# First feed-forward layer: Strassen products accumulated in the banks of the first and fifth product, with snapshots by ScalarE

## The chip, the core and the metric

The kernel runs on one core of a Trainium2 chip. The metric is the device time of one execution in microseconds (us); lower is better. The engines are named as the profile names them: PE is TensorE (matmuls; PEld its weight loads), DVE is VectorE, ACT is ScalarE, POOL is GpSimd, and SP is the queue that issues most DMAs. SBUF is the memory on the core from which the engines work; PSUM is the small memory into which TensorE writes its results, in eight banks of 512 fp32 values for each of 128 partitions.

## The reference

Attention within hash buckets for 4 batches x 8 heads x 768 tokens x 64, then a two-layer feed-forward network over 3072 tokens:

```python
mask = q_bucket[:, :, :, None] == k_bucket[:, :, None, :]
scores = np.where(mask, scale * np.matmul(q, k.transpose(0, 1, 3, 2)), -1000000000.0)
attn = softmax(scores)                       # over the keys
x = (attn @ v).transpose(0, 2, 1, 3)         # to (3072, 512)
h = x @ w_in                                 # w_in is (512, 2048)
g = h * (1.0 / (1.0 + np.exp(-1.702 * h)))
out = g @ w_out                              # w_out is (2048, 512)
```

The change is in the line that computes `h`, and in how `g` is taken from it. All arithmetic is fp32.

## The kernel before

**Three stages.** Attention fills `xT`, the transposed input of the network, until 316 us. Then the first layer runs until 605 us and writes `g` and sums of it to DRAM (`g_dram`). The second layer reads them back with `fetch` into `raw_g` and a part of `s_in`, and ends at 868 us.

**The first layer.** Tokens are cut in three blocks of 1024 (`sb`), the 2048 columns of `w_in` in eight pairs of 128 (`mt`). One call of `hidden(sb, mt)` makes one tile, that is, four results of 128 x 512: `u` (c11), `c12`, `c21` and `c22`, a 2 x 2 block product. It is made in the manner of Strassen and Winograd, with seven products instead of eight. Product `i` multiplies the weight quarter `LEFT[i]` with the token quarter `RIGHT[i]`; quarters 0 to 3 are parts of `w_in_sb` or `xT`, quarters 4 to 6 sums of them (`s_in` on the weights' side, `t_x` on the tokens' side). `K2` is 2, and in the profile each fp32 matmul of the program appears as two instructions, so a product is four matmul instructions of 128 x 128 x 512.

**The results of a tile**, with p1 to p7 for the products:

```
u   = p1 + p2
v   = p1 + p6
c21 = v + p7 + p4
c22 = v + p7 + p5
c12 = v + p5 + p3
```

Before the change every product has a PSUM bank of its own, which `bank()` hands out from a pool of six (`f0`; two more, `f1`, are added from tile 21 on; tiles are counted from 0 to 23). ScalarE copies p1 to `u`, and VectorE makes the other sums, each with one operand from PSUM. Then `emit` applies the activation on ScalarE (`Gelu_apprx_sigmoid`, L732) and `keep` issues the store to DRAM (L729). After the four results, POOL makes four sums for the next layer (`sums_b`, L219 to L222), which are stored too.

**What else runs in a tile.** `mid` and `end` are lists of steps that are put into the order of the engines within a tile: the sums of tokens for the next block (`sums_b(nc.vector, *quarters_x(sb + 1))`, L219 to L222 on VectorE), the conversion of `w_out` from its 64-bit form (L180 to L198 on VectorE, with a Square on ScalarE at L190, reading `raw`, which a DMA at L162 loads), sums of `w_out` quarters in the last block (`sums_a`, L211 to L214, on VectorE and POOL), and the first loads and sums of the second layer (`fetch`, L791; `g_sums`).

**What sets the order.** TensorE, VectorE, ScalarE and POOL run their instructions in the order in which the program issues them (`manual_schedule`). The DMAs on SP are put in order by a planner, by the times at which it expects their conditions to be met. Buffers of the pool `stage` (`u`, `v`, `c12`, `c21`, `c22`) exist twice, `t2` and `t4` once.

The first tile, `hidden(0, 0)`, is issued from the end of attention (`next(ff)`), before the last normalization of `xT`.

Of the kernel before, what the change touches and what calls it, by code (L numbers as in the profile page):

```python
# [8 lines left out]
F32 = mybir.dt.float32  # L9
# [3 lines left out]
Act = mybir.ActivationFunctionType  # L13
Alu = mybir.AluOpType
# [5 lines left out]
P = 128  # L20
# [18 lines left out]
def kernel(  # L39
# [17 lines left out]
    nc = tc.nc  # L57
# [8 lines left out]
    KC, FC = DM // P, FF // P  # L66
# [149 lines left out]
    def sums_b(eng, b11, b12, b21, b22, t1, t2, t4):  # L216


        return [lambda: eng.tensor_tensor(t1, b12, b11, op=Alu.subtract),  # L219
                lambda: eng.tensor_tensor(b12, b22, b12, op=Alu.subtract),  # L220
                lambda: eng.tensor_tensor(t2, b22, t1, op=Alu.subtract),  # L221
                lambda: eng.tensor_tensor(t4, b21, t2, op=Alu.subtract)]  # L222

    K2, F2 = KC // 2, FF // 2
    XT = 512

    def quarters_in(cols):
        w = [w_in_sb[:, K2 * k : K2 * (k + 1), F2 * i + cols.start : F2 * i + cols.stop]
             for i in range(2) for k in range(2)]
        return w + [s_in[:, i, :, cols] for i in range(3)]  # L230

    def quarters_x(sb):
        x = [xT[:, K2 * k : K2 * (k + 1), (2 * sb + j) * XT : (2 * sb + j + 1) * XT] for k in range(2) for j in range(2)]
        return x + [t_x[:, i] for i in range(3)]
# [460 lines left out]
    def feed_forward(tag, late=()):  # L695
# [4 lines left out]
        n1 = N // (2 * XT)  # L700

        LEFT = dict(zip(range(1, 8), (0, 1, 6, 3, 4, 5, 2)))
        RIGHT = dict(zip(range(1, 8), (0, 2, 3, 6, 4, 5, 1)))
        OUTER = (1, 2, 6, 7, 5, 3, 4)
        with ExitStack() as fctx:
            stage_ctx = fctx.enter_context(ExitStack())
            stage = stage_ctx.enter_context(tc.tile_pool(name=f"stage{tag}", bufs=2, side="right"))
# [4 lines left out]
            def bank():  # L712
                turn[0] += 1
                return sets[turn[0] % 8 // 6 if len(sets) > 1 else 0].tile([P, XT], F32, tag="p", name="product")

            def hidden(sb, mt, mid=(), end=()):
                u, v, c12, c21, c22 = (stage.tile([P, XT], F32, tag=x, name=x) for x in ("u", "v", "c12", "c21", "c22"))
                t2, t4 = (stage.tile([P, XT], F32, tag=x, name=x, bufs=1) for x in ("t2", "t4"))
                wq, xq = quarters_in(slice(mt * P, (mt + 1) * P)), quarters_x(sb)

                def product(i):
                    ps = bank()
                    for kc in range(K2):
                        nc.tensor.matmul(ps, wq[LEFT[i]][:, kc, :], xq[RIGHT[i]][:, kc, :],  # L724
                                         start=(kc == 0), stop=(kc == K2 - 1))
                    return ps

                def keep(at, x):
                    loader[0].dma_start(out=g_dram[len(LEFT) * sb + at, :, mt, :], in_=x)  # L729

                def emit(c, at=None):
                    nc.scalar.activation(c, c, Act.Gelu_apprx_sigmoid)  # L732
                    if at is not None:
                        keep(at, c)

                nc.scalar.copy(u, product(1))
                nc.vector.tensor_tensor(v, product(6), u, op=Alu.add)
                nc.vector.tensor_tensor(c21, product(7), v, op=Alu.add)
                p = product(5)
                nc.vector.tensor_tensor(c22, p, c21, op=Alu.add)  # L740
                emit(c22, 3)
                nc.vector.tensor_tensor(c12, p, v, op=Alu.add)
                nc.vector.tensor_tensor(u, product(2), u, op=Alu.add)
                emit(u, 0)
                for x in mid:
                    x()
                nc.vector.tensor_tensor(c12, product(3), c12, op=Alu.add)
                emit(c12)
                nc.vector.tensor_tensor(c21, product(4), c21, op=Alu.add)
                emit(c21, 2)  # L750

                for f, kept in zip(sums_b(nc.gpsimd, u, c12, c21, c22, v, t2, t4), ((4, v), (1, c12), (5, t2), (6, t4))):
                    f()
                    keep(*kept)
                for x in end:
                    x()
# [129 lines left out]
            for sb in range(n1):  # L886
                for mt in range(MT):
                    n = sb * MT + mt
# [36 lines left out]
                    x = sums_b(nc.vector, *quarters_x(sb + 1)) if mt == MT - 1 and sb + 1 < n1 else []  # L925
                    t = {3 * MT - 2: g_sums(0)[:2], 3 * MT - 1: g_sums(0)[2:]}.get(n, []) if n > 3 * MT - 3 else []
                    hidden(sb, mt, x[:3] + ([lambda: fetch(1)] if n == 3 * MT - 1 else []), x[3:] + t + todo.pop(n, []))
                    yield
            stage_ctx.close()
# [58 lines left out]
    def whole(steps):  # L988
        for _ in steps:
            pass  # L990

    ff = feed_forward("", in_chunks[len(in_chunks) - LATE :])
    attention(ff)
    whole(ff)
# [5 lines left out]
    with tc.If(unsafe, preferred_fallthrough_block=False):  # L1000
        with tc.tile_pool(name="cv3", bufs=1) as cv:
            for x in in_chunks:
                whole(convert(cv, *x))
        for f in in_sums(0):
            f()
        shifted_attention()
        for f in sums_b(nc.vector, *quarters_x(0)):
            f()
        whole(feed_forward("2"))
# [27 lines left out]
```

## Time and profile before

| | |
|---|---|
| median of 3 runs | 870.38 us (870.25 to 870.49) |
| span of the profiled execution | 868.1 us; no own time is shown beside it |
| mean granted clock of TensorE | 0.996 |
| first layer | 316.4 to 605.2 us |
| one product of the first layer | 4 matmuls, start to start 1.717 us |
| copy of a product by ScalarE (L736) | 24 times, mean 583 ns |
| activation of a result (L732) | 96 times, mean 630 ns |
| add with one operand from PSUM on VectorE (L737 to L749) | 7 x 24 times, 681 to 692 ns |
| sum of two SBUF operands of 128 x 512 on POOL (L219 to L222) | means 1311 to 1388 ns in the first layer |

A row of the timeline has the start, the duration, the engine, the line of the kernel, the operation with its result and operands, and in brackets for how long the engine was idle before it and which instruction ended that. Matmuls overlap in the pipeline, so that four of them that start 0.429 us apart are shown as 1.88 us.

### The profile page before, as it was taken

Reading aid. Unit: us, or ns where it says so; the run is one execution under the profiler, and the core shown is the slowest. Engines: PE = TensorE matmul, PEld = TensorE weight load, DVE = VectorE, ACT = ScalarE, POOL = GpSimd, SP = SyncE. Lnnn points to the kernel's source line nnn. Section 1 sums busy time; section 2 is a strip of 40 time slices with the busy share of each in tenths; the row PEclk is TensorE's granted clock in tenths of the full one; section 3 lists DMA queues with packets and bytes.
Section 4 is the critical chain, followed back from the end, with each engine's and each line's share of the span. In section 5 each row is a group of like instructions: output and inputs, shape, how many; then the busy total and the mean of one; then the engine's idle time right before and its main releaser. Section 6 shows DMA issues by size and latency. Waiting matters only on the chain.

```text
span 868.1 us, 13473 instructions
## 1 busy us (share of the span) xinstructions
PE 857.6 (99%) x4845; PEld 499.7 (58%) x4845; DVE 719.2 (83%) x1020; ACT 313.4 (36%) x519; POOL 313.6 (36%) x275
## 2 busy tenths in 40 slices
PE   9999999999999999999999999999999999999996
PEld 5444444444444444444444444444888888888885
DVE  4589999999999887778777778888888977897786
ACT  5866667777666643322233322332000000000000
POOL 4243223334323566665544344659904100000000
PEclk9999999999999999999999999999999999999998
DMA  5636645446552205556455555575844685467524
GB/s 126 97 56 109 107 85 85 85 89 122 98 101 61 62 2 188 186 196 212 175 195 186 189 193 194 194 251 180 301 161 154 201 246 197 162 208 242 194 98 100
DMA packets 169162, 132.10 MB, mean 152 GB/s; under 512 B 123616, under 2 KB 138112, under 8 KB 163712
## 3 DMA queue, kind: packets, MB, share of 16 engines
q1 hardware_dynamic: 166528, 129.70, 52.3%
q10 hardware_dynamic: 2560, 1.46, 0.8%
q8 instruction: 40, 0.66, 0.3%
q14 instruction: 34, 0.28, 0.1%
HBM read 79.69 MB, written 50.33 MB: 150 GB/s over the span
## 4 chain that ended last, share of the span: by engine, by line
PE 97%; DVE 2%; DMA 0%; issue 0%; ACTq 0%; ACT 0%; DVEq 0%
PE product L724 33%; PE product L836 27%; PE ps L432 18%; PE av L465 15%; PE dn L486 1%; PE hash L408 1%; DVE xT L840 1%; PE tp L366 1%; DVE y L816 1%; DMA k<-in_k_dram 0%; PE hash L373 0%; DVE v L840 0%; DVE t2a L221 0%; DVE raw_g L220 0%; ACTq L823 0%
## 5 line engine op out<-in xcount | busy, mean ns | idle before, releaser
L433 ACT ACTIVATE e<-ps 128x768 f32<-128x768 f32 x192 | 151.2, 812 | 25.6 <-PE ps L432 23.0
L432 PE MATMUL ps<-qT,kT 64*128 64x384 f32 x768 | 155.1, 482 | 0.0
L724 PE MATMUL product<-xT,w_in_sb 128*128 128x512 f32 x288 | 135.5, 593 | 0.0
L465 PE MATMUL av<-e,v 128*32 128x385 f32 x1536 | 128.0, 487 | 0.0
L440 POOL TENSOR_TENSOR acc<-e 128x768 f32<-128x768 f32 x32 | 51.8, 1619 | 194.4 <-ACT e L433 174.9
L732 ACT ACTIVATE c<-c 128x512 f32<-128x512 f32 x72 | 45.4, 630 | 186.6 <-issue 78.5
L724 PEld LDWEIGHTS product<-xT,w_in_sb 128*128 128x128 f32 x288 | 54.7, 190 | 69.0 <-issue 64.4
L465 PEld LDWEIGHTS av<-e,v 128*32 128x32 f32 x1536 | 48.6, 109 | 76.2 <-issue 73.8
L724 PE MATMUL product<-t_x,s_in 128*128 128x512 f32 x192 | 90.2, 592 | 0.0
L432 PEld LDWEIGHTS ps<-qT,kT 64*128 64x128 f32 x768 | 68.0, 188 | 38.5 <-issue 38.4
L219 POOL TENSOR_TENSOR v<-c,u 128x512 f32<-128x512 f32 x24 | 34.2, 1423 | 122.3 <-ACT c L732 122.3
L849 ACT COPY u<-product 128x256 f32<-128x256 f32 x21 | 7.8, 372 | 172.1 <-PE product L836 138.9
L432 PE MATMUL ps<-qf,kf 64*128 64x384 bf16 x384 | 62.9, 324 | 0.1
L724 PEld LDWEIGHTS product<-t_x,s_in 128*128 128x128 f32 x192 | 36.5, 190 | 45.9 <-issue 43.3
L441 POOL TENSOR_TENSOR acc<-acc,e 128x768 f32<-128x768 f32 x32 | 55.9, 1746 | 2.5
L446 DVE SCALAR_TENSOR_TENSOR acc<-e 128x768 f32<-128x768 f32 x32 | 47.7, 1492 | 5.1 <-ACT e L433 5.1
L724 PE MATMUL product<-xT,s_in 128*128 128x512 f32 x96 | 45.1, 592 | 0.0
L724 PE MATMUL product<-t_x,w_in_sb 128*128 128x512 f32 x96 | 45.1, 592 | 0.0
L432 PEld LDWEIGHTS <-kf 64*128 64x128 bf16 x384 | 19.0, 94 | 35.1 <-DMA q<-in_q_dram 6.2
L448 DVE TENSOR_TENSOR acc<-acc,e 128x768 f32<-128x768 f32 x32 | 34.3, 1072 | 3.3
L448 DVE TENSOR_TENSOR acc<-acc,acc 128x768 f32<-128x768 f32 x32 | 31.2, 974 | 6.3 <-POOL acc L441 3.2
L836 PE MATMUL product<-raw_g,xT 128*128 128x256 f32 x152 | 35.1, 379 | 0.0
(207 smaller groups left out, 1498.5 us busy)
## 6 DMA issues: line engine op xcount, KB each, us to landing
raw_g<-g_dram SPq DMA_DIRECT2D x22, 1024.0 KB
s_in<-g_dram SPq DMA_DIRECT2D x20, 1024.0 KB
g_dram<-c SPq DMA_DIRECT2D x72, 256.0 KB
g_dram<-t SPq DMA_DIRECT2D x48, 256.0 KB
raw<-in_moe_w_in_dram SPq DMA_DIRECT2D x16, 512.0 KB
raw<-in_moe_w_out_dram SPq DMA_DIRECT2D x16, 512.0 KB
v<-in_v_dram SPq DMA_DIRECT2D x32, 192.0 KB
g_dram<-u SPq DMA_DIRECT2D x24, 256.0 KB
```

Of the source, the lines that this page charges most:

```text
L219: return [lambda: eng.tensor_tensor(t1, b12, b11, op=Alu.subtract), lambda: eng.tensor_tensor(b12, b22, b12, op=Alu.subtract), lambda: eng ...
L366: nc.tensor.matmul(tp[D * j : D * (j + 1), i * P : (i + 1) * P], x[name][:, j, c * GT + i, :], ident, start=True, stop=True)
L432: nc.tensor.matmul(ps[:, j, 0:HS], a[hs, keys], m[hs, cols], start=not last, stop=last)
L433: nc.scalar.activation(es[c][:, kt, :, 0:HS], ps[:, :, 0:HS], Act.Exp, scale=1.0 / D**0.5)
L440: nc.gpsimd.tensor_tensor(acc, es[c][:, 0, :, 0:HS], es[c][:, 1, :, 0:HS], op=Alu.add)
L441: nc.gpsimd.tensor_tensor(acc, acc, es[c][:, 2, :, 0:HS], op=Alu.add)
L446: nc.vector.scalar_tensor_tensor(acc, e[0], T * TINY, e[1], op0=Alu.add, op1=Alu.add)
L448: nc.vector.tensor_tensor(acc, acc, x, op=Alu.add)
L465: nc.tensor.matmul(av[D * j + d : D * j + d + 32, :], vt[:, t, j, d : d + 32], es[c][:, t, j, :], start=(t == 0), stop=(t == T - 1))
L724: nc.tensor.matmul(ps, wq[LEFT[i]][:, kc, :], xq[RIGHT[i]][:, kc, :], start=(kc == 0), stop=(kc == K2 - 1))
L732: nc.scalar.activation(c, c, Act.Gelu_apprx_sigmoid)
L836: nc.tensor.matmul(ps, wq[LEFT[i]][:, c, :], gq[RIGHT[i]][:, c, :], start=(c == 0), stop=(c == F4 - 1))
```

## The change

The products no longer have a bank each. Product 1 starts bank `a`; product 6, then 7, then 4 are accumulated on top of it, and ScalarE takes a snapshot between them: after p1 (`u`), after p6 (`v`) and after p7 (into `c22`). The activation of c21 reads bank `a` itself. Product 5 starts bank `b`, and product 3 is accumulated onto it. Product 2 has a bank `c`. VectorE is left with three adds out of PSUM per tile: c22, u and c12. Product 1 of a tile and its copy are issued by `head`, in the middle of the tile before, except for the very first tile. The order of products was 1, 6, 7, 5, 2, 3, 4; it becomes 6, 5, 7, 2, product 1 of the next tile, 4, 3. The activation of c21 now comes before that of c12.

```diff
+            def product(ps, sb, mt, i, start=True):
+                wq, xq = quarters_in(slice(mt * P, (mt + 1) * P)), quarters_x(sb)
+                for kc in range(K2):
+                    nc.tensor.matmul(ps, wq[LEFT[i]][:, kc, :], xq[RIGHT[i]][:, kc, :],
+                                     start=(start and kc == 0), stop=(kc == K2 - 1), skip_group_check=not start)
+
+            def head(n):
+                ps, u = bank(), stage.tile([P, XT], F32, tag="u", name="u")
+                product(ps, *divmod(n, FC // 2), 1)
+                nc.scalar.copy(u, ps)
+                return ps, u
+
+            heads = {}
+
             def hidden(sb, mt, mid=(), end=()):
...
+                n = sb * (FC // 2) + mt
+                a, u = heads.pop(n) if n in heads else head(n)
...
-                def emit(c, at=None):
-                    nc.scalar.activation(c, c, Act.Gelu_apprx_sigmoid)
+                def emit(c, at=None, of=None):
+                    nc.scalar.activation(c, c if of is None else of, Act.Gelu_apprx_sigmoid)
                     if at is not None:
                         keep(at, c)
 
-                nc.scalar.copy(u, product(1))
-                nc.vector.tensor_tensor(v, product(6), u, op=Alu.add)
-                nc.vector.tensor_tensor(c21, product(7), v, op=Alu.add)
-                p = product(5)
-                nc.vector.tensor_tensor(c22, p, c21, op=Alu.add)
+                product(a, sb, mt, 6, False)
+                nc.scalar.copy(v, a)
+                b = bank()
+                product(b, sb, mt, 5)
+                product(a, sb, mt, 7, False)
+                nc.scalar.copy(c22, a)
+                nc.vector.tensor_tensor(c22, b, c22, op=Alu.add)
                 emit(c22, 3)
-                nc.vector.tensor_tensor(c12, p, v, op=Alu.add)
-                nc.vector.tensor_tensor(u, product(2), u, op=Alu.add)
+                c = bank()
+                product(c, sb, mt, 2)
+                nc.vector.tensor_tensor(u, c, u, op=Alu.add)
                 emit(u, 0)
+                if n + 1 < n1 * (FC // 2):
+                    heads[n + 1] = head(n + 1)
                 for x in mid:
                     x()
-                nc.vector.tensor_tensor(c12, product(3), c12, op=Alu.add)
+                product(a, sb, mt, 4, False)
+                emit(c21, 2, a)
+                product(b, sb, mt, 3, False)
+                nc.vector.tensor_tensor(c12, b, v, op=Alu.add)
                 emit(c12)
-                nc.vector.tensor_tensor(c21, product(4), c21, op=Alu.add)
-                emit(c21, 2)
```

More of the change, by code (lines that the diff above doesn't have):

```diff
@@ L716, in hidden @@
+            heads = {}
             def hidden(sb, mt, mid=(), end=()):
-                u, v, c12, c21, c22 = (stage.tile([P, XT], F32, tag=x, name=x) for x in ("u", "v", "c12", "c21", "c22"))
+                n = sb * (FC // 2) + mt
+                a, u = heads.pop(n) if n in heads else head(n)
+                v, c12, c21, c22 = (stage.tile([P, XT], F32, tag=x, name=x) for x in ("v", "c12", "c21", "c22"))
                 t2, t4 = (stage.tile([P, XT], F32, tag=x, name=x, bufs=1) for x in ("t2", "t4"))
-                wq, xq = quarters_in(slice(mt * P, (mt + 1) * P)), quarters_x(sb)
@@ L721, in product @@
[L721 to L726, printed above, removed]
                 def keep(at, x):
                     loader[0].dma_start(out=g_dram[len(LEFT) * sb + at, :, mt, :], in_=x)
-                def emit(c, at=None):
-                    nc.scalar.activation(c, c, Act.Gelu_apprx_sigmoid)
+                def emit(c, at=None, of=None):
+                    nc.scalar.activation(c, c if of is None else of, Act.Gelu_apprx_sigmoid)
```

## The prediction

> **What bounds the kernel now.** I read the page first, parts 1 and 4, and then the busy time of the three stages: attention, first layer (316.4 to 605.2 us), second layer.
>
> ```profile
> PE 857.6 (99%) x4845; PEld 499.7 (58%) x4845; DVE 719.2 (83%) x1020; ACT 313.4 (36%) x519; POOL 313.6 (36%) x275
> PE 97%; DVE 2%; DMA 0%; issue 0%; ACTq 0%; ACT 0%; DVEq 0%
> 316.40:605.20 288.80, 288.80 (x680) 127.92 (x673) 231.03 (x307) 84.55 (x141) 161.28 (x133) 1.00 0.53 188
> ```
>
> The chain that ended last is TensorE almost throughout. In the windows line the columns are the stretch, then busy time of PE, PEld, DVE, ACT and POOL, granted clock, DMA share and GB/s: TensorE has no gap in the stage that is changed, at granted clock 1.00. Busy time can hide short gaps, so I check it by starts: a product is 4 matmul instructions and starts 1.717 us after the one before (320.24, 321.96, 323.68 in the timeline); 24 tiles x 7 products x 1.717 = 288.5 us, which is 605.21 minus 316.70. Nothing is left over. The second layer is as full: 21 steps x 7 products x 8 matmuls x 0.2158 us (1.727 per product) = 253.8 of the 254.2 us from 605.21 to 859.4. So VectorE, 80% busy in the first layer, holds nobody up, and all the idle time that any relief of it could return is about 0.4 us.
>
> Next, the timeline of a steady tile and of the first one. Columns: start, duration, engine, line, what.
>
> ```profile
> 425.16 0.69 DVE L749 TENSOR_TENSOR c<-product,c 128x512 f32<-128x512 f32 x1 [1.02 <-PE product L724]
> 425.93 0.63 ACT L732 ACTIVATE c<-c 128x512 f32<-128x512 f32 x1 [1.14 <-DVE c L749]
> 426.47 0.63 ACT L190 ACTIVATE size<-raw 128x512 f32<-128x512 f32 x1
> 427.03 0.59 ACT L736 COPY u<-product 128x512 f32<-128x512 f32 x1
> ```
> ```profile
> 316.70 1.98 PE L724 MATMUL product<-xT,w_in_sb 128*128 128x512 f32 x4
> 318.53 1.88 PE L724 MATMUL product<-t_x,s_in 128*128 128x512 f32 x4
> 318.77 0.58 ACT L736 COPY u<-product 128x512 f32<-128x512 f32 x1 [0.44 <-PE product L724]
> 319.37 1.28 ACT L732 ACT_TABLE_LOAD   x1
> 323.09 0.68 DVE L737 TENSOR_TENSOR v<-product,u 128x512 f32<-128x512 f32 x1
> ```
>
> In the first fence the product before ended at 424.96: DVE adds 0.20 us after a product's end, Gelu starts 0.97 after it, the conversion's Square 1.51 after it, and the copy out of PSUM ends 2.66 after it. In the second, product 6 of the first tile starts at 318.53, before the copy of product 1 has begun. Today it may: it has its own bank.
>
> **The change, part by part.** *Arithmetic moved.* Seven VectorE adds out of PSUM a tile (L737 to L749, 0.68 to 0.69 us) become three: 4 x 0.69 x 24 = 66 us less, 231 to about 165 us. ScalarE gets two more copies a tile of 0.58 us (L736): 28 us more, 84.6 to about 112 of 289. TensorE keeps 7 products of 4 matmuls; three of the four add into their bank already and all start 0.429 us apart, so a fourth that adds costs nothing. Worth on the end: 0, since neither engine is the bound.
>
> *New waits of TensorE.* Products 6, 7 and 4 now go into product 1's bank, each after a snapshot by ScalarE; product 3 into product 5's after VectorE has read it. The order becomes 6, 5, 7, 2, product 1 of the next tile, 4, 3. I set the start of product 6 at 0; the products then start at 0, 1.72, 3.43, 5.15, 6.87, 8.58, 10.30, and the next tile at 12.02.
> - 7 waits for the copy of v. By the first fence, with product 3's end in the place of 424.96, that copy ends at 2.66, behind Gelu and Square. Product 7's first weight load (0.19 us) must start by 3.24. Slack 0.58: cost 0. On ScalarE only the copy of c22, not due before 5.35, is queued behind it.
> - 4 waits for the copy of c22, done at about 5.35 + 0.59 = 5.94, and is due at 8.58: cost 0.
> - 3 waits for the add of c22. VectorE first does the six conversion steps (425.77 to 430.86, 5.1 us), 0.8 to 5.9, then this add, to 6.7; due at 10.30: cost 0.
> - 6 of the next tile waits for its u, copied 8.78 to 9.4, due 12.02: cost 0. At the end of a token block the three block sums (1.22 us each, 410.32 to 413.93) end 0.73 us before product 6 starts, now as before, because in both orders three products lie between the end of product 2, which starts them, and product 6: cost 0.
>
> *First tile.* Nothing precedes its head, so 6 directly follows 1 and must wait for the copy, which ends at 318.77 + 0.58 = 319.35. It restarts at about 319.40 (a wait on VectorE at 683.10 was followed by a matmul 0.14 later; I take 0.05 to 0.14), against 318.53: 0.87 to 0.96. A product whose weights could not be loaded ahead loses 0.11 more (316.70 to 318.53 is 1.83, not 1.72). Sum 1.0 us, with nothing to hide it, as TensorE is full behind it. The table load slides behind the copy of c22 and delays only Gelu. VectorE's backlog up to 323.09 no longer matters: the first add is due after product 7.
>
> *Tile 21 to 22.* VectorE runs four long sums (581.98 to 590.0, 8.0 us; up to 8.7 if POOL overlaps all of them at the 2.2 us that the overlapped ones take). They now start 0.82 after product 6 and end at 8.8 to 9.5; two adds, Gelu and Gelu, then the next u is copied by 11.5 to 12.1, needed at 11.83: 0 to 0.3. I take 0.1.
>
> *POOL and the queues.* The Gelu of c12 is now behind the tile's last product instead of two products earlier, so POOL's four sums (L219 to L222, 5.1 us) and the stores of v, c, t on SP come 1.60 after product 6 instead of 1.8 before it: 3.4 later. In a steady tile they end at 6.7; their buffers are wanted at 12 or later: cost 0. The next raw load sits behind them on SP (issued 430.54, right after the t stores); issued at about 7.2 instead of 3.9, used at 12.9, it has 5.7 us; 512 KB at the 225 to 287 GB/s of 431 to 434 us take 2, some 3 with the stores beside them: cost 0. At the end of the stage POOL is busy without a break from 581 to 629, and slides by 3.4 + 1.0:
>
> ```profile
> 600.82 1.67 SPq L729 DMA_DIRECT2D g_dram<-t  x2
> 600.87 1.27 POOL L222 TENSOR_TENSOR t<-c,t 128x512 f32<-128x512 f32 x1
> 602.58 0.88 SPq L791 DMA_DIRECT2D s_in<-g_dram  x2
> 610.99 2.01 DVE L219 TENSOR_TENSOR t_x<-s_in 128x1024 f32<-128x1024 f32 x1 [1.22 <-DMA s_in<-g_dram]
> 618.55 1.62 DVE L221 TENSOR_TENSOR t_x<-s_in,t_x 128x1024 f32<-128x1024 f32 x1
> 622.48 1.89 PE L836 MATMUL product<-t_x,w_in_sb 128*128 128x256 f32 x8
> ```
>
> The load of s_in follows the t stores on SP, VectorE waits for it, and TensorE needs the third sum 2.3 us after it is done. In the new order the load's own condition, product 5 of the last tile, comes earlier in the tile and the t stores later, so I expect the planner to put it ahead of those stores and it to go out near 602.5 as now: 0. If it stays behind them: rival two. The next load (615.92, used at 629.4, 6.8 us of traffic) can lose 4 us and keep 3.
>
> Sum: 1.0 + 0.1 = +1.1 us on a span of 868.1. No own time is shown beside that span; the runs' median of 870.38 lies 2.3 above it, taken as the unchanged surroundings. Forecast 871.5, own range 870.8 to 872.1.
>
> The Trainium skill (TensorE: Matmul & The Clock Gate, "A second HAM failure mode: psum-queue depth-cycling") speaks against this change: brief idling between groups while cycling through PSUM banks made the clock of another kernel fall and recover. This trace shows no fall within 2 us:
>
> ```profile
> 3.00:4.00 1.00, 0.66 (x2) 1.00 0.77 175
> 860.00:861.00 1.00, 0.00 (x0) 1.00 0.73 138
> 862.00:863.00 1.00, 0.00 (x0) 0.50 0.94 239
> ```
>
> The third number from the right is the clock; TensorE's last matmul ended at 859.6. One stop of 1 us keeps full clock by these rows. If it did not, each product at 0.50 would take 1.7 us more, and two of them give 874.9: rival three.
>
> **The rivals.** *One, slower: the copy of v comes late.* Place: product 7 of the 18 tiles with a conversion, where Square stands before the copy. It decides from 0.58 us of lateness, by a Square that waits for its raw load or a slower answer from ScalarE to TensorE. If it came 0.8 late: 18 x 0.22 = 4.0 us, 875.5; with 0.65 late, 1.3 and 872.8. For: the longest round trip now inside a tile, without spare banks. Against: every link is measured above, and that raw load keeps 2.7 us. Chance 0.20.
>
> *Two, slower: s_in comes late.* POOL ends tile 22's sums near 606 to 607 and the load goes behind the stores: 4 to 5 us later, so VectorE's first sum starts at 615 to 616, the third ends 8.8 us of work later at about 624.5, where TensorE wants it at 623.3: 1 to 2 us on top, 872.5 to 873.5. Chance 0.14.
>
> *Three, the clock falls* after stops: 874.9. Chance 0.02.
>
> *Four, faster: VectorE was the brake.* 66 us of its work goes; if TensorE had been held by it, the time would drop. The starts leave 0.4 us at most, 870.0, which would not be told from no change; more would need a matmul pitch under 0.429. Chance of a real gain 0.02.
>
> **How the numbers follow.** About 0.2% (1.74 us) is what a measurement of this kernel can tell from no change, so same means 868.6 to 872.1. The forecast has 0.62. Its start-up term could grow by a few tenths and cross the bound; I give 0.06 of it to slower. Same 0.56; slower 0.06 + 0.20 + 0.14 + 0.02 = 0.42; faster 0.02. The range reaches from 870.5 to 874.2: the forecast, rival two and the lower half of rival one.
>
> **What would show it.** Right: no 318.53 start, product 6 of the first tile near 319.4; products 1.717 us apart elsewhere; VectorE in the stage near 165 us, ScalarE near 112. Wrong: gaps before product 7 or 6 in every tile (rival one), a TensorE gap near 623 (two), a clock under 1.00 before 860 (three), or a pitch under 1.717 (four).

## The result, and the profile after

The changed kernel takes 872.97 us (median of 8 runs, 871.47 to 873.69) against 870.32 (8 runs) for the kernel before: 2.65 us slower, ratio 1.0031, 95% interval 1.0021 to 1.0041. The forecast was 871.5 and "no change" as the likeliest case. The measured time lies in the range of 870.5 to 874.2, but past the upper bound of "same" (872.1): the likeliest case was not the one that came. The profiled execution took 872.87 us, 1.9 more than its span of 871.0.

The page of the changed kernel, parts 1 and 4, then the busy time of the first layer's stretch:

```profile
PE 857.9 (99%) x4845; PEld 499.2 (57%) x4845; DVE 661.4 (76%) x924; ACT 340.2 (39%) x567; POOL 311.6 (36%) x275
PE 95%; DVE 3%; issue 0%; DMA 0%; ACT 0%; ACTq 0%; DVEq 0%
```
```profile
316.40:605.20 288.80, 287.99 (x674) 127.33 (x671) 171.78 (x211) 111.11 (x189) 155.81 (x129) 1.00 0.55 189
```

VectorE lost 58 us of work over the span, ScalarE gained 27, and TensorE's busy time is the same to 0.3 us. The span grew by 2.9 all the same, and the share of VectorE in the chain that ended last went from 2% to 3%. So TensorE stood still somewhere, and waits of TensorE are the view to ask next (waiting instruction, releaser, us in total, times, longest):

```profile
PE product L851 <- DVE t2a L221: 1.7, 1, 1.7
PE warm L359 <- DVE idle L76: 1.2, 1, 1.2
PE product L719 <- ACT u L726: 0.8, 1, 0.8
```

The second of these was there before. Two are new, each a single stop: one of 0.8 us in the first layer (L719), one of 1.7 in the second (L851), far from the edited lines. The first, in the timeline:

```profile
316.59 1.98 PE L719 MATMUL product<-xT,w_in_sb 128*128 128x512 f32 x4
...
318.65 0.58 ACT L726 COPY u<-product 128x512 f32<-128x512 f32 x1 [0.45 <-PE product L719]
...
319.38 3.67 PE L719 MATMUL product<-t_x,s_in 128*128 128x512 f32 x8 [0.81 <-ACT u L726]
```

Product 6 of the first tile starts 2.79 us after product 1 instead of 1.83: 0.96 us late, behind the copy. The layer lasts 289.55 us from its first product to the first of the second layer (606.14), against 288.51: 1.04 us more. The missing 0.08 lies directly behind the stop, where products 6 and 5 take 3.51 us (319.38 to 322.89) instead of 2 x 1.717; after that nothing is lost.

The second stop is in the third step of the second layer. Rows of VectorE, POOL and TensorE in the order of time:

```profile
627.52 1.07 DVE L855 TENSOR_TENSOR v<-v,xT 128x256 f32<-128x256 f32 x1
628.52 2.89 DVE L855 TENSOR_TENSOR xT<-xT 128x256 f32<-128x256 f32 x2
...
631.21 1.33 POOL L214 TENSOR_TENSOR w_in_sb<-xT,w_in_sb 128x512 f32<-128x512 f32 x1
631.34 1.48 DVE L855 TENSOR_TENSOR xT<-xT,v 128x256 f32<-128x256 f32 x1
632.75 1.21 DVE L219 TENSOR_TENSOR t1a<-raw_g 128x1024 f32<-128x1024 f32 x1
...
633.77 1.89 PE L851 MATMUL product<-raw_g,w_in_sb 128*128 128x256 f32 x8
...
636.01 1.21 DVE L221 TENSOR_TENSOR t2a<-raw_g,t1a 128x1024 f32<-128x1024 f32 x1
637.37 1.97 PE L851 MATMUL product<-t2a,w_in_sb 128*128 128x256 f32 x8 [1.71 <-DVE t2a L221]
```

The t2a product should start 1.73 us after 633.77, at 635.50; it starts at 637.37, 1.87 late, when VectorE has made t2a. VectorE is late because four adds of 128 x 256 took 5.4 us (1.07, 2.89 for two, 1.48); such an add takes 0.42 us when POOL is idle. POOL ends its last sum only at 632.54. The same place before the change:

```profile
626.59 1.18 DVE L840 TENSOR_TENSOR v<-v,xT 128x256 f32<-128x256 f32 x1
627.57 1.33 POOL L214 TENSOR_TENSOR w_in_sb<-xT,w_in_sb 128x512 f32<-128x512 f32 x1
...
627.70 1.94 DVE L840 TENSOR_TENSOR xT<-xT 128x256 f32<-128x256 f32 x2
...
629.55 0.42 DVE L840 TENSOR_TENSOR xT<-xT,v 128x256 f32<-128x256 f32 x1
...
633.16 1.22 DVE L221 TENSOR_TENSOR t2a<-raw_g,t1a 128x1024 f32<-128x1024 f32 x1
...
634.56 1.92 PE L836 MATMUL product<-t2a,w_in_sb 128*128 128x256 f32 x8
```

There POOL ended at 628.90, the four adds took 3.5 us, and t2a was done at 634.38, 0.18 us before its product. The two stops together, 1.04 + 1.87 = 2.91 us, are the whole difference between the two spans (871.0 - 868.1 = 2.9).

### The profile page after: what moved, and what is told of

It reads as the page before. It is cut to its first block, busy times and chain, and to the rows that moved or that the text cites. A ratio compares the mean times of both kernels' runs of the same rounds, so it can differ in the third digit from the quotient of the medians.

```text
span 871.0 us, 13350 instructions
## 1 busy us (share of the span) xinstructions
PE 857.9 (99%) x4845; PEld 499.2 (57%) x4845; DVE 661.4 (76%) x924; ACT 340.2 (39%) x567; POOL 311.6 (36%) x275
## 4 chain that ended last, share of the span: by engine, by line
PE 95%; DVE 3%; issue 0%; DMA 0%; ACT 0%; ACTq 0%; DVEq 0%
PE product L719 33%; PE product L851 26%; PE ps L432 18%; PE av L465 15%; DVE xT L855 1%; PE dn L486 1%; PE hash L408 1%; PE tp L366 1%; DVE y L831 1%; DMA k<-in_k_dram 0%; DVE v L855 0%; PE hash L373 0%; DVE t2a L221 0%; DVE raw_g L220 0%; ACTq L838 0%
## 5 line engine op out<-in xcount | busy, mean ns | idle before, releaser
L719 PE MATMUL product<-xT,w_in_sb 128*128 128x512 f32 x288 | 127.8, 592 | 0.0
L719 PEld LDWEIGHTS product<-xT,w_in_sb 128*128 128x128 f32 x288 | 54.6, 190 | 69.0 <-issue 68.5
L719 PE MATMUL product<-t_x,s_in 128*128 128x512 f32 x192 | 86.4, 592 | 0.8 <-ACT u L726 0.8
L764 DVE TENSOR_TENSOR c<-product,v 128x512 f32<-128x512 f32 x24 | 16.6, 690 | 90.8 <-PE product L719 90.8
L219 POOL TENSOR_TENSOR v<-c,u 128x512 f32<-128x512 f32 x24 | 32.3, 1345 | 128.1 <-ACT c L741 128.1
L719 PEld LDWEIGHTS product<-t_x,s_in 128*128 128x128 f32 x192 | 36.4, 190 | 47.1 <-issue 45.2
L741 ACT ACTIVATE c<-c 128x512 f32<-128x512 f32 x48 | 30.3, 630 | 72.3 <-DVE c L764 43.7
L719 PE MATMUL product<-t_x,w_in_sb 128*128 128x512 f32 x96 | 45.1, 592 | 0.0
L719 PE MATMUL product<-xT,s_in 128*128 128x512 f32 x96 | 45.1, 592 | 0.0
L750 ACT COPY c<-product 128x512 f32<-128x512 f32 x24 | 14.1, 586 | 66.3 <-PE product L719 66.3
```

The source lines that it names most:

```text
L741: nc.scalar.activation(c, c if of is None else of, Act.Gelu_apprx_sigmoid)
L764: nc.vector.tensor_tensor(c12, b, v, op=Alu.add)
```

## The experiments

My theory was that the two stops are all that the change costs; that the first comes from the first tile's order; and that the second comes from POOL: its sums start later in each tile, so at the end of the first layer its queue ends later, beside VectorE's adds. The rival for the second stop was the load of `s_in`, which VectorE awaits longer than before:

```profile
597.75 0.32 SPq L806 DMA_DIRECT2D s_in<-g_dram  x1
...
607.17 0.40 SPq L806 DMA_DIRECT2D s_in<-g_dram  x1
...
612.89 2.27 DVE L219 TENSOR_TENSOR t_x<-s_in 128x1024 f32<-128x1024 f32 x1 [2.18 <-DMA s_in<-g_dram]
```

The medians of the experiments belong to two later series, in which the kernel before takes 869.82 us (`e1` to `e4`) and 869.38 us (`e5` to `e8`). They are compared by their ratios to it, and above all by the positions in their traces.

**POOL's last four sums of this stretch issued later** (`e1_pool_later`).

```diff
-                if n in (5, 6):
+                if n in (3, 5, 6):
                     nc.gpsimd.tensor_copy(mark, ms[OUTER[n - 1]][0:1, 0, 0:1])
-                for f in {0: inner_sums(4), 5: ...
+                for f in {3: inner_sums(4), 5: ...
```

> The changed kernel, with one thing moved: POOL's four sums for the fifth step of the second layer (inner_sums(4)) are issued at the fourth step, behind a one-element copy that waits for the third step's result, instead of right behind the others at about 627 to 632.5 us. Theory (POOL's slide): in the changed kernel POOL works 3.6 us longer beside VectorE, whose adds between 628.5 and 632.8 take 1.4 us each instead of 0.42, so t2a is 1.87 us late for TensorE. Then POOL ends near 627, VectorE's adds are short again, the stop before the t2a product is gone, and the time is 872.97 - 1.87 = 871.1 us (870.9 to 871.4). Rival (the load of s_in): the lateness stems from the load that VectorE awaits 2.18 us instead of 1.22 at 610.7; this run leaves that load as it is, so the stop stays at 1.9 and the time at 873.0.

Measured: ratio 1.0016 (1.0007 to 1.0026), that is 1.4 us over the kernel before instead of 2.7. Its trace:

```profile
613.56 2.22 DVE L219 TENSOR_TENSOR t_x<-s_in 128x1024 f32<-128x1024 f32 x1 [2.22 <-DMA s_in<-g_dram]
...
626.44 1.26 POOL L214 TENSOR_TENSOR w_in_sb<-w_out_sb,w_in_sb 128x512 f32<-128x512 f32 x1
...
628.15 0.43 DVE L855 TENSOR_TENSOR v<-v,xT 128x256 f32<-128x256 f32 x1
628.49 0.88 DVE L855 TENSOR_TENSOR xT<-xT 128x256 f32<-128x256 f32 x2
629.29 0.42 DVE L855 TENSOR_TENSOR xT<-xT,v 128x256 f32<-128x256 f32 x1
...
633.82 1.22 DVE L221 TENSOR_TENSOR t2a<-raw_g,t1a 128x1024 f32<-128x1024 f32 x1
...
636.12 1.89 PE L851 MATMUL product<-t2a,w_in_sb 128*128 128x256 f32 x8
```

The wait for `s_in` is as long as in the changed kernel (2.22), and the stop is gone: the rival falls. The same four adds take 1.7 us instead of 5.4 once POOL has ended at 627.70, t2a is done 1.1 us before TensorE wants it, and the t2a product starts 29.35 us after the second layer's first product, exactly as before the change (634.56 - 605.21). The first stop, of 0.81, is still there.

**The first tile in another order** (`e2_first_tile`): one product between 1 and 6, one between 6 and 7.

```diff
+                b, c = bank(), bank()
+                if n == 0:
+                    product(b, sb, mt, 5)
                 product(a, sb, mt, 6, False)
                 nc.scalar.copy(v, a)
-                b = bank()
-                product(b, sb, mt, 5)
+                product(*((c, sb, mt, 2) if n == 0 else (b, sb, mt, 5)))
                 product(a, sb, mt, 7, False)
...
-                c = bank()
-                product(c, sb, mt, 2)
+                if n > 0:
+                    product(c, sb, mt, 2)
```

> The changed kernel, with the first tile's products in the order 1, 5, 6, 2, 7, head of the next, 4, 3, so that one product lies between 1 and 6 and one between 6 and 7. The start-up theory: the stop of 0.81 us and 0.15 of lost overlap before product 6 (319.38 instead of 318.42) vanish, and the first layer ends 0.96 earlier. The second stop depends on POOL and VectorE relative to TensorE: POOL's work moves with the tiles, so it stays at 1.9, and the time is 872.0 (871.7 to 872.4). If POOL's slide is set by something that does not move with the tiles, the second stop grows by 0.96 and the time stays at 873.0.

Measured: ratio 1.0018 (1.0009 to 1.0027), 1.5 us over the kernel before. The layer lasts 288.51 us again, so the first stop is gone to the last hundredth. The second is unchanged: the t2a product starts at 31.22 us of the second layer, as in the changed kernel (31.23). So POOL's lateness moves with the tiles, and each stop stays as it is when the other goes.

**Both edits** (`e3_both`).

> Both edits together: POOL's sums of inner_sums(4) at the fourth step, and the first tile's order 1, 5, 6, 2, 7. If the two stops are all that the change cost, both are gone: 873.0 - 0.96 - 1.87 = 870.15 us, the same as before (870.32) within 0.3, with the first layer ending near 605.2 and no stop of TensorE over 0.3 us after 317. If a third cost is hidden, 870.8 or more.

Measured: ratio 1.0004 (0.9995 to 1.0013), not to be told from the kernel before. The layer lasts 288.50 us, and product 6 of the first tile and the t2a product start without a wait:

```profile
318.87 3.60 PE L719 MATMUL product<-t_x,s_in 128*128 128x512 f32 x8
...
634.90 1.89 PE L853 MATMUL product<-t2a,w_in_sb 128*128 128x256 f32 x8
```

No third cost shows; by the interval one of up to 1.1 us could go unseen in the time, but the trace has no place for it. With both stops removed the change costs nothing that can be measured, and it brings nothing either, though VectorE has a quarter less to do in the layer.

**Products 3 and 4 exchanged in the changed kernel** (`e4_three_first`), which brings c12, and with it POOL's sums, one product forward.

```diff
-                product(a, sb, mt, 4, False)
-                emit(c21, 2, a)
                 product(b, sb, mt, 3, False)
                 nc.vector.tensor_tensor(c12, b, v, op=Alu.add)
                 emit(c12)
+                product(a, sb, mt, 4, False)
+                emit(c21, 2, a)
```

> The changed kernel with products 3 and 4 exchanged, so that c12, which POOL's first sum waits for, is done one product earlier. POOL's slide theory: POOL's sums start 1.7 us earlier in each tile, POOL ends near 630.8 instead of 632.5, VectorE has 1.7 us less of overlap and the stop before the t2a product shrinks from 1.9 to between 0.3 and 1.2: 871.4 to 872.3 us. The rival that s_in is late: the stop stays, 873.0. A side effect: Gelu of c21 reads PSUM 0.2 us after the tile's last product and no longer waits for VectorE, so the copy of v is not later than now; no new stops in the tiles are expected.

Measured: ratio 1.0017 (1.0008 to 1.0026), 1.5 us over the kernel before. POOL ends earlier and most of the second stop goes:

```profile
630.01 1.33 POOL L214 TENSOR_TENSOR w_in_sb<-xT,w_in_sb 128x512 f32<-128x512 f32 x1
...
636.50 1.97 PE L851 MATMUL product<-t2a,w_in_sb 128*128 128x256 f32 x8 [0.23 <-DVE t2a L221]
```

The t2a product starts at 636.50 instead of 636.11 (1.727 after the product before it at 634.38): 0.39 late, within the 0.3 to 1.2 that I had expected.

**The slide without the accumulation** (`e6_before_c12_last`): the kernel before, with c12 made last.

```diff
-                nc.vector.tensor_tensor(c12, product(3), c12, op=Alu.add)
-                emit(c12)
                 nc.vector.tensor_tensor(c21, product(4), c21, op=Alu.add)
                 emit(c21, 2)
+                nc.vector.tensor_tensor(c12, product(3), c12, op=Alu.add)
+                emit(c12)
```

> The kernel before, with only products 3 and 4 (with their adds, activations and stores) exchanged, so that c12 comes last: POOL's sums slide by one product, 1.72 us, and nothing is accumulated across products. Theory (POOL's slide alone makes the second stop): POOL ends about 25.4 us after the start of the second layer instead of 23.7; with 24.6 (products 3 and 4 exchanged in the changed kernel) the stop before the t2a product was 0.4 and with 26.4 it was 1.9, so here 0.7 to 1.3 us: 871.0 to 871.6 against 870.3 before. Rival (the stop comes from the accumulation, the snapshots or the load of s_in): no stop, 870.3.

Measured: ratio 1.0009 (0.9999 to 1.0018). The interval just takes in no change, so the time alone does not decide; the trace does:

```profile
628.41 1.33 POOL L214 TENSOR_TENSOR w_in_sb<-xT,w_in_sb 128x512 f32<-128x512 f32 x1
...
634.90 1.97 PE L836 MATMUL product<-t2a,w_in_sb 128*128 128x256 f32 x8 [0.20 <-DVE t2a L221]
```

The same stop appears in a kernel that accumulates nothing across products, 0.36 us long. I had expected 0.7 to 1.3, because I let POOL slide by a whole product; it slid by 0.9 only. POOL's end against the start of the second layer orders all the runs in which POOL works without a break through that start to these sums:

| kernel | POOL ends | t2a product starts | late by |
|---|---|---|---|
| before | 23.69 | 29.35 | 0 |
| changed, product 7 behind product 6 (last experiment) | 23.97 | 29.59 | 0.24 |
| before, c12 last | 24.55 | 29.71 | 0.36 |
| changed, products 3 and 4 exchanged | 24.58 | 29.74 | 0.39 |
| changed, other first tile | 26.40 | 31.22 | 1.87 |
| changed | 26.40 | 31.23 | 1.88 |

(us from the second layer's first product). The lateness grows with POOL's end, though not in proportion. The two kernels near 24.6 have the same lateness to 0.03, one with accumulation and one without. So it is POOL's time, and not the accumulation, that makes the stop.

**POOL's sums later in the kernel before** (`e8_before_pool_later`): the first edit above, made to the kernel before.

> The kernel before, with only POOL's inner_sums(4) moved to the fourth step. Theory: in the kernel before t2a is done 0.2 us before TensorE wants it, so there is no stop to save: 0 to 0.1 us faster, not to be told from no change. If POOL's overlap with VectorE cost the kernel before something too, it is faster by more.

Measured: ratio 1.0004 (0.9995 to 1.0013). t2a is done at 27.33 us instead of 29.17, two microseconds before its product, and nothing is faster: before, t2a came just in time.

**Three edits** (`e7_three_edits`): other first tile, products exchanged, POOL's sums later.

> The changed kernel with all three edits: first tile in the order 1, 5, 6, 2, 7; products 3 and 4 exchanged; POOL's inner_sums(4) at the fourth step. TensorE is then without a stop, as with two edits, so the exchange has nothing left to save: the same as the kernel before within 0.5 us. If a cost was still hidden in POOL's slide, this is faster than with two edits by some tenths.

Measured: ratio 1.0003 (0.9994 to 1.0012). TensorE has no stop in it in either layer. It is no better than the kernel before; with TensorE's starts as close as they were, none of these versions can be.

**Product 7 directly behind product 6** (`e5_adjacent`), to measure the hand-over that product 5 covers.

```diff
                 product(a, sb, mt, 6, False)
                 nc.scalar.copy(v, a)
                 b = bank()
-                product(b, sb, mt, 5)
                 product(a, sb, mt, 7, False)
                 nc.scalar.copy(c22, a)
+                product(b, sb, mt, 5)
```

> The changed kernel with product 7 directly behind product 6 (order 6, 7, 5, 2, head, 4, 3), so that nothing covers the snapshot between them. It measures the hand-over from TensorE to ScalarE and back. Theory (the cover by product 5 is what makes the change nearly free): product 6 ends at 1.72, the copy of v ends at about 2.5 (2.66 where a Square is ahead), product 7 starts 0.14 later instead of at 1.72, and loses 0.11 more for weights not loaded ahead: 1.0 to 1.2 us a tile, 24 to 29 us over 24 tiles; 896 to 902 us. Rival (TensorE does not wait for the snapshot in a way that costs, since the bank is split or the wait is short): under 5 us.

Measured: 895.56 us (two runs), ratio 1.030 (1.028 to 1.032). The longest wait of TensorE, and a window over the layer and the start of the next:

```profile
PE product L719 <- ACT v L746: 18.1, 24, 0.8
```
```profile
316.00:650.00 334.00, 315.08 (x773) 142.65 (x766) 189.13 (x227) 113.83 (x194) 177.73 (x143) 1.00 0.52 180
```

All 24 tiles stop. The layer lasts 314.07 us (630.93 - 316.86) instead of 289.55, 1.02 us a tile; 0.75 of it is shown as idle, and the rest I take for lost overlap. The total came out 0.4 below the 896 to 902 that I had expected. Two things lower it: in this series the kernel before is 0.9 us faster than in the first, and the second stop shrank to 0.24 (29.59 in the table).

## Why the prediction was right, and where it was wrong

**Right: what bounds the kernel.** No gain came from 58 us less on VectorE; the pitch of 1.717 us is unchanged and the layer lost only what the first tile lost, 1.04 us.

**Right: the steady tile.** The slack before product 7 holds. In a tile with a conversion the copy of v ends 2.59 us after the start of product 6 (forecast 2.66):

```profile
427.61 3.60 PE L719 MATMUL product<-t_x,s_in 128*128 128x512 f32 x8
...
429.63 0.57 ACT L746 COPY v<-product 128x512 f32<-128x512 f32 x1
```

In 24 tiles there is not one stop behind product 5, and without that cover each tile costs 1.02 us. Rival one (a late copy of v) did not happen. ScalarE is at 111 us in the stretch (112 forecast), VectorE at 172 (165 forecast).

**Right: the first tile.** Forecast 1.0 us; product 6 starts 0.96 late and the layer ends 1.04 later. The other order removes exactly that.

**Too careful: tile 21 to 22.** The 0.1 us taken for the four long sums is 0. The next u is copied by 594.81 and product 6 starts at 595.84.

**Wrong: "POOL and the queues", the term of POOL at the end of the stage, mis-sized at 0; it measured 1.87 us.** The slide itself was forecast, and larger than it was (4.4 us; POOL ended 3.64 later by the clock of the trace, 2.71 later against the second layer). What I checked was who waits for POOL's results and for the stores behind them, and all of those had cover. What I did not check was who works beside POOL. In the profile of before the answer was there: the adds at 626 to 630 already took up to 1.18 us, POOL ended at 628.90, and the t2a product at 634.56 started 0.18 us after t2a was done. Even that was hardly cover: in the five runs in which this product is late, it starts 0.14 to 0.15 us after t2a is done, which leaves some 0.03 us. I weighed only the sum that TensorE wants at 622.48, with its 2.3 us of cover, and not t2a, which it wants at 634.56. With almost no cover there, most of each us of POOL beside those adds goes to the end: by the table, 1.88 us of lateness for 2.71 us of POOL.

The Trainium skill states the mechanism (SBUF — State Buffer, "Who interferes with whom"): a VectorE instruction with two SBUF inputs contends with a GpSimd instruction that reads SBUF, and one with at most one SBUF input, outside the two-port modes, does not. The traces agree: in the changed kernel the four adds of two SBUF operands take 1.07 to 1.48 us beside POOL and such an add takes 0.42 without it, while those with one operand from PSUM stay at 0.41 to 0.42 either way.

**The last load, kept less than forecast.** That paragraph of the prediction left the next load of `raw_g` 3 us to spare. In the run with POOL's sums later (`e1_pool_later`) VectorE waits for it, and it comes 0.4 us before TensorE starts on `raw_g` at 630.95:

```profile
630.55 1.23 DVE L219 TENSOR_TENSOR t1a<-raw_g 128x1024 f32<-128x1024 f32 x1 [0.84 <-DMA raw_g<-g_dram]
```

It cost nothing in any run, but by less than the forecast said.

**Rival two (s_in late) named the wrong place.** The first half of the load did go ahead of the stores, at 597.75, as forecast, but the second half went out only at 607.17, behind them; before the change both halves were issued from 602.58 on. VectorE's wait grew by only 1.0 us, and no stop of TensorE follows at 623.41.

**Luck: the range.** The sum's own range of 870.8 to 872.1 does not hold the result. The wider range does, but its upper part was drawn for rivals one and two. Neither came, and the stop at t2a, which no rival named, filled their place.

**Rival three (the clock).** The granted clock stays at 1.00 in every microsecond of the layer in the run with 24 stops of about 0.75 us. The rule of the Trainium skill that the prediction weighed (TensorE: Matmul & The Clock Gate, "A second HAM failure mode: psum-queue depth-cycling") does not show in this kernel.

## What to carry to other kernels

Where one engine was full from start to end, taking work from another brought nothing; ask first for the bound engine's idle time, which was 0.4 us here. A step that ends later than before must be checked twice: for who waits for its result, and for who works beside it and becomes slower, down to the smallest cover along the new overlap, which here lay some 30 us behind the last edited instruction. In this kernel, accumulating in a bank across snapshots was free where another product lay between a product and its successor in the bank, and cost 1 us each time where none did; the first tile, without a predecessor, needs an order of its own.

## What I had not expected of the hardware

The same VectorE add of two SBUF operands of 128 x 256 took 0.42 us alone and up to 1.48 us beside POOL, 3.5 times as long, while POOL's sum of 128 x 512 beside it took 1.33 to 1.44 instead of 1.27. Where both engines worked on longer operands, both slowed: VectorE's sum of 128 x 1024 from 1.22 to 2.2 us and POOL's from 1.27 to 2.2. So where the adds were small, they paid nearly all of the price.
